# Clustered attention, dense layer and routed experts on one core: conversions respaced, preparation one step later, expert relu on one engine, two splits moved

## The chip, the cores and the metric

The program runs on one core of a Trainium2 chip. A core has five engines with a queue each that runs strictly in order: PE (TensorE, matrix products and transposes), DVE (VectorE), ACT (ScalarE), POOL (GpSimd) and SP (SyncE, which here only issues DMA transfers). Engines wait for one another through semaphores. The metric is the device time of one launch in microseconds (us), and lower is better.

## The reference

```python
def _attn_ref(q, k, v, centroids):          # q, k, v: 2 x 8 heads x 768 x 64; 16 centroids a head
    q_assign = np.argmax(np.einsum('bhsd,hcd->bhsc', q_n, c_n), axis=-1)   # and k_assign
    mask = q_assign[:, :, :, None] == k_assign[:, :, None, :]
    scores = np.where(mask, scale * np.matmul(q, k.transpose(0, 1, 3, 2)), -1000000000.0)
    attn = np.exp(scores - np.max(scores, axis=-1, keepdims=True))
    return np.matmul(attn / (np.sum(attn, axis=-1, keepdims=True) + 1e-09), v)
...
h = x @ w_in                                 # x: 1536 tokens x 512, w_in: 512 x 2048
x = np.maximum(0.01 * h, h) @ w_out          # w_out: 2048 x 512
...
# then 8 experts: each token with x @ w_skip > 0 goes to the expert with the largest logit
h = np.maximum(xc[mask] @ w1[e], 0.0)        # w1[e]: 512 x 1024
y[mask] = gate_w[mask, None] * (h @ w2[e])   # w2[e]: 1024 x 512
out[do_compute] = xc + y
```

`w_in` and `w_out` come as 64-bit floating-point numbers, and the kernel turns them into 32-bit ones itself.

## The kernel before

The kernel has three parts, and its order is written out by hand: the framework adds the semaphores but moves nothing, so the order of the code is the order on every engine.

**Attention.** Two heads form a pair, and there are 8 pairs with 12 steps each (96 steps, `s`; within a pair the step is `r`, within half a pair `rf`). One step computes the scores of 128 queries of one head (`st_scores`), takes their maximum on DVE, the exponential on ACT (`st_exp`), and, three steps later (`LAG`), transposes the result on PE (`st_transpose`, two PSUM buffers `tps`) and copies it out of PSUM on ACT (`st_evac`, tile `pt`). In every second step eight products with `v` follow (`st_av`). After each half of a pair `recip_rows` transposes the reciprocals of the row sums into one of the same two PSUM buffers (`rcps`), ACT copies them out, SP stores them, and `recip_load` on POOL's queue reads them back for `av_split`, which writes the attention output as a rounded part `xh` and a rest `xl`. While a pair is computed, the next ones are prepared: `raw_pe`/`raw_act` transpose q and k, `assign_*`, `argmax_*` and `mask_*` find the clusters. The tables `PREP`, `PREP0`, `PREP1` and `PREPS` give step and slot of each piece; `plan(d)` makes such a table, in which `d` is the step of the last argmax operation. The preparing products share one PSUM buffer.

**Conversion.** `w_in` and `w_out` come in 32 pieces. A piece is loaded (`load_piece`, tiles `stg`), and `convert_op` turns it with one operation on ACT (tile `cvu`) and four on DVE into 32-bit numbers. Twenty pieces are done during attention (`conv_step`), the last twelve in the first layer (`conv_next(n)`: convert, two pieces at a time, until `n` of the twelve are done).

**The first layer** goes over three blocks of 512 tokens (`NBLK`, `BT`) and in each over 16 slices of the hidden width (`NFC`); `i` counts all 48. Every operand is split into a rounded part and a rest, and three products stand for one. `m1_up(i)` makes 12 products into `ups`; `m1_act(i)` is the chain ACT `lk`, DVE `g`, ACT `gh`, DVE `gl`; `m1_down(i)` makes 12 products into `acc`. The weights of slice `i + 2` are split by `split_i(i + 2)` (ACT `whii`, then POOL `wloi`) and `split_o(i + 2)` (ACT `whio`, POOL `wloo`), which stand behind `m1_act(i)` in the code. The route of each block's tokens is computed beside it (`r_trans`, `r_part`, `r_logit`, `r_gen`).

**The experts.** The 36 weight pieces of 1 MB ("chunks") go through a ring of eight (`rawa` two, `rawb` six). An expert has four stages, two up (`up_half`) and two down (`down_half`); `split_stage(n)` splits the chunk of stage `n` into his two parts with two ACT copies and two subtractions (`split2`), writes them over the used `xh` and `xl`, and then asks for the next chunk (`refill`). Stage `n + 3` (`LEAD`) is split while PE computes stage `n`. After `up_half` the relu of half 0 is on ACT and that of half 1 on DVE; `h_trans` transposes it, ACT makes `hTh` and DVE `hTl`. `extras` and `tile_list` are some 60 small DVE operations between the first stages, which find the tokens that exceed one tile of 128.

## Time and profile before

| what | value |
|---|---|
| median of 3 runs | 690.68 us (690.42 to 690.96) |
| the profiled execution | 689.63 us, its span 687.9 us |
| PE / ACT / DVE / POOL busy, share of the span | 93% / 62% / 59% / 40% |
| attention / first layer / experts, by where their work stands in the trace | to 266 / 266 to 555 / 566 to 680 us |

The span reaches from the first to the last instruction of the profiled execution; the rest of its time, 1.73 us, lies outside. A busy PE is only an upper bound of its use, since the ends of its instructions are modelled; what counts is where it starts late and what released it.

### The profile page before, as it was taken

The numbers are of one execution on the slowest core, as the hardware profiler recorded it, in microseconds if no ns is written. First come the engines' busy times: TensorE is split into PE (matmuls) and PEld (weight loads), VectorE is DVE, ScalarE is ACT, GpSimd is POOL, SyncE is SP. The second block draws the span as 40 slices with busy tenths as digits, with TensorE's granted clock in tenths as the row PEclk, the third lists the DMA queues.
The fourth block names the chain that finished last, engine by engine and source line by source line (L and its number), as shares of the span: only waits on it lengthen the run. The fifth ranks groups of instructions, "written<-read, shape, count | busy, mean of one in ns | idle before, by whom it ended". The sixth has DMA issues, their size and how long they took to land. (4 is left out here: it accounts for less than half of the span.)

```text
span 687.9 us, 10140 instructions
## 1 busy us (share of the span) xinstructions
PE 636.7 (93%) x3587; PEld 491.8 (71%) x3587; DVE 407.4 (59%) x687; ACT 423.8 (62%) x824; POOL 278.2 (40%) x295
## 2 busy tenths in 40 slices
PE   5898999999999999499999999999999979989994
PEld 3676766666766666378888888788787868767873
DVE  5755858686776653767523213623226348999991
ACT  5887888897888885254445444445444436757870
POOL 4233636264553324363554444444444273002321
PEclk9999999999999999889999999999999999999997
DMA  8763764767656354221003000006303349989950
GB/s 196 184 189 95 196 163 140 187 172 193 167 153 171 111 183 144 104 111 61 1 3 122 1 1 0 1 0 245 122 3 122 123 163 362 339 280 333 357 192 25
DMA packets 62659, 98.31 MB, mean 143 GB/s; under 512 B 27593, under 2 KB 31659, under 8 KB 62224
## 3 DMA queue, kind: packets, MB, share of 16 engines
q1 hardware_dynamic: 59040, 88.13, 41.5%
q0 software_dynamic: 3568, 9.52, 4.2%
q8 instruction: 29, 0.48, 0.3%
q14 instruction: 22, 0.18, 0.1%
HBM read 72.47 MB, written 11.65 MB: 122 GB/s over the span
## 5 line engine op out<-in xcount | busy, mean ns | idle before, releaser
L369 DVE TENSOR_REDUCE st<-sps 128x1 f32<-128x768 f32 x96 | 91.5, 954 | 66.7 <-PE sps L366 66.3
L430 ACT ACTIVATE pt<-tps 128x384 f32<-128x384 f32 x192 | 84.8, 503 | 19.2 <-PE tps L423 18.6
L384 ACT ACTIVATE pr<-sps,st 128x768 f32<-128x768 f32 x96 | 87.7, 914 | 13.9 <-DVE st L369 13.4
L750 DVE TENSOR_TENSOR g<-ups,lk 128x512 f32<-128x512 f32 x48 | 33.1, 689 | 105.9 <-ACT lk L749 105.8
L634 POOL TENSOR_TENSOR wloi<-rawb,whii 128x512 fp32r<-128x512 f32 x36 | 46.7, 1298 | 115.4 <-ACT whii L632 115.4
L658 PE MATMUL ups<-xh,whii 128*128 128x512 f32 x192 | 76.0, 396 | 7.9 <-ACT whii L632 7.9
L423 PE MATMUL tps<-ident,pr 128*128 128x128 f32 x576 | 78.7, 273 | 0.5 <-ACT pt L430 0.5
L658 PE MATMUL ups<-xh,wloi 128*128 128x512 f32 x192 | 75.7, 394 | 1.4 <-POOL wloi L634 1.3
L658 PE MATMUL ups<-xl,whii 128*128 128x512 f32 x192 | 75.6, 394 | 0.0
L765 PE MATMUL acc<-whio,gh 128*128 128x512 f32 x184 | 73.4, 399 | 0.0
L765 PE MATMUL acc<-wloo,gh 128*128 128x512 f32 x184 | 71.8, 390 | 0.1
L423 PEld LDWEIGHTS tps<-ident,pr 128*128 128x128 f32 x576 | 68.4, 140 | 5.1 <-ACT pt L430 1.6
L438 PE MATMUL avps<-pt,vnat 128*64 128x384 f32 x384 | 71.9, 498 | 0.0
L765 PE MATMUL acc<-whio,gl 128*128 128x512 f32 x184 | 71.8, 390 | 0.0
L751 ACT ACTIVATE gh<-g 128x512 fp32r<-128x512 f32 x48 | 30.4, 632 | 51.9 <-DVE g L750 51.9
L749 ACT ACTIVATE lk<-ups 128x512 f32<-128x512 f32 x48 | 28.5, 593 | 50.9 <-PE ups L658 50.9
L752 DVE TENSOR_TENSOR gl<-g,gh 128x512 fp32r<-128x512 f32 x48 | 34.6, 721 | 33.5 <-ACT gh L751 33.5
L453 POOL TENSOR_TENSOR xr<-xr,rb 128x384 f32<-128x384 f32 x16 | 16.0, 1002 | 81.2 <-ACT xr L446 77.9
L658 PEld LDWEIGHTS ups<-xh,whii 128*128 128x128 f32 x192 | 36.6, 190 | 16.3 <-ACT whii L632 8.3
L644 POOL TENSOR_TENSOR wloo<-rawb,whio 128x512 fp32r<-128x512 f32 x36 | 47.0, 1304 | 0.8 <-ACT whio L643 0.8
L1171 POOL DMA_INDIRECT out_dram<-y,idx_s x8 | 13.6, 1695 | 76.8 <-DVE y L1169 36.0
L658 PEld LDWEIGHTS ups<-xh,wloi 128*128 128x128 f32 x192 | 36.6, 190 | 10.2 <-POOL wloi L634 2.6
(294 smaller groups left out, 1388.8 us busy)
## 6 DMA issues: line engine op xcount, KB each, us to landing
rawb<-in_moe_w_dram SPq DMA_DIRECT2D x26, 1024.0 KB, 6.9
stg<-in_moe_w_in_dram SPq DMA_DIRECT2D x16, 512.0 KB
stg<-in_moe_w_out_dram SPq DMA_DIRECT2D x16, 512.0 KB, 6.8
rawa<-in_moe_w_dram SPq DMA_DIRECT2D x8, 1024.0 KB
vnat<-in_v_dram SPq DMA_DIRECT2D x8, 384.0 KB, 3.7
rb<-recip_scratch POOLq DMA_DIRECT2D x32, 96.0 KB, 3.0
w_f_scratch<-cvt SPq DMA_DIRECT2D x12, 256.0 KB, 2.3
rawb<-w_f_scratch SPq DMA_DIRECT2D x3, 1024.0 KB
```

The source lines that it names most:

```text
L369: nc.vector.tensor_reduce(out=st[:, 0:1], in_=ps[:, :, 0:HS], axis=AX.XY, op=ALU.max, negate=True)
L384: nc.scalar.activation(out=pr, in_=ps[:, :, 0:HS], func=AF.Exp, bias=st[:, 0:1], accum_out=sm_t[g][:, 3 * h + j:3 * h + j + 1])
L423: nc.tensor.transpose(ps[:, t, :], pr[:, kh, t * P:(t + 1) * P], ident)
L430: nc.scalar.activation(out=pt[:, 3 * kh:3 * kh + 3, j, :], in_=t_t[s][kh], func=AF.Copy)
L438: nc.tensor.matmul(av_t[g][64 * h:64 * h + 64, :], lhsT=vnat[p][:, h, kt, :], rhs=pt_t[p, half, h][:, kt].rearrange("p j c -> p (j c)"), s ...
L634: eng.tensor_tensor(out=lo, in0=src, in1=_f(hi), op=ALU.subtract)
L644: nc.gpsimd.tensor_tensor(out=lo, in0=src, in1=_f(hi), op=ALU.subtract)
L658: nc.tensor.matmul(ps, lhsT=w[:, cc, :], rhs=x[:, cc, cs], start=(n == 0), stop=(n == 3 * KD - 1))
L750: nc.vector.tensor_tensor(out=g, in0=ps, in1=t, op=ALU.max)
L751: nc.scalar.activation(out=gh, in_=g, func=AF.Copy)
L752: nc.vector.tensor_tensor(out=gl, in0=g, in1=_f(gh), op=ALU.subtract)
L765: nc.tensor.matmul(ps, lhsT=a[:, ts_], rhs=w, start=(fc == 0 and n == 0), stop=(fc == NFC - 1 and n == 2))
```

## The change

1. `plan(0)` becomes `plan(1)` for the pairs 4 to 7, `plan(4)` becomes `plan(5)` for pair 2 and `plan(2)` becomes `plan(3)` for pair 3: transposes, assignment and argmax of the next pair stand one step later. `recip_rows` and the store of its row also stand one step later (`rf` 3 and 4 instead of 2 and 3).
2. `xh` and `xl` are laid out by block instead of by token. `av_split` makes two pieces of each half pair that crosses a block's edge (8 of 16 halves).
3. The twelve pieces left for the first layer are converted two each at `i` = 1, 3, 5, 7, 8, 9. Before it was four at `i` = 1 and two each at 3, 5, 7, 9.
4. Stages 0 and 1 of the experts are split at `i` = 37 and 40 of the first layer, with DVE's subtraction in place of POOL's, and their chunks' successors are loaded there by SP. Stage 2 takes the place of stage 0 behind the layer (POOL), stage 3 that of stage 2 (DVE). The chunks 12 and 13 are loaded ahead of 10 and 11.
5. Both halves of the experts' relu are on ACT.
6. The one-hot matrix of `tile_list` is made by 4 DVE operations over three tiles instead of 12 over one.

```diff
@@ -320,12 +320,12 @@
             (3, "d", exchange, 0), (5, "d", exchange, 1), (max(d + 2, 5), "d", mask_dma, None),
         ]
 
-    PREP = plan(0)
+    PREP = plan(1)
     PREP0 = [(3, "a0", assign_act, None), (3, "pb", argmax_pe, None), (4, "d", argmax_0, None), (4, "d", argmax_1, None),
              (5, "d", argmax_2, None), (6, "d", argmax_3, None)]
     PREP1 = [(1, "pb", assign_pe, None), (2, "a0", assign_act, None), (2, "pb", argmax_pe, None), (3, "pb", argmax_0, None), (4, "pb", argmax_1, None), (5, "d", argmax_2, None), (6, "pb", argmax_3, None), (7, "pb", mask_pe, None), (8, "d", mask_dve, None),
              (8, "d", mask_dma, None)]
-    PREPS = {0: PREP0, 1: PREP1, 2: plan(4), 3: plan(2)}
+    PREPS = {0: PREP0, 1: PREP1, 2: plan(5), 3: plan(3)}
 
     def prep(p, r, slot):
         if p >= NP:
@@ -341,8 +341,11 @@
 
     NP = B * NPAIR
 
-    xh = xpool.tile([P, KD, NTOK], F32R, name="xh")
-    xl = xpool.tile([P, KD, NTOK], F32R, name="xl")
+    NBLK = 3
+    BT = NTOK // NBLK
+    TPB = BT // P
+    xh = xpool.tile([P, NBLK, KD, BT], F32R, name="xh")
+    xl = xpool.tile([P, NBLK, KD, BT], F32R, name="xl")
 
     NSTEP = B * NPAIR * 12
     rcs = [att.tile([P, P], F32, name=f"rc{i}") for i in range(2)]
@@ -448,11 +451,18 @@
     def av_split(g):
         p, half = divmod(g, 2)
         b, cc = divmod(p, NPAIR)
-        cs = slice(b * S + half * HS, b * S + (half + 1) * HS)
         xr = xr_t.pop(g)
         nc.gpsimd.tensor_tensor(out=xr, in0=xr, in1=rrow_t.pop(g), op=ALU.mult)
-        nc.gpsimd.tensor_scalar(out=xh[:, cc, cs], in0=xr, scalar1=1.0, scalar2=1.0, op0=ALU.mult, op1=ALU.mult)
-        nc.gpsimd.tensor_tensor(out=xl[:, cc, cs], in0=xr, in1=_f(xh[:, cc, cs]), op=ALU.subtract)
+        n0 = b * S + half * HS
+        cuts = sorted({n0, n0 + HS} | {n for n in range(0, NTOK, BT) if n0 < n < n0 + HS})
+        parts = []
+        for a, z in zip(cuts, cuts[1:]):
+            blk = a // BT
+            cs = slice(a - blk * BT, z - blk * BT)
+            parts.append((xr[:, a - n0:z - n0], xh[:, blk, cc, cs], xl[:, blk, cc, cs]))
+        for src, hi, lo in parts:
+            nc.gpsimd.tensor_scalar(out=hi, in0=src, scalar1=1.0, scalar2=1.0, op0=ALU.mult, op1=ALU.mult)
+            nc.gpsimd.tensor_tensor(out=lo, in0=src, in1=_f(hi), op=ALU.subtract)
 
     def first_copy(i):
         nm = "qk"[i // 2]
@@ -617,9 +627,6 @@
                 if m + 2 < NPC:
                     load_piece(*divmod(m + 2, 4))
 
-    NBLK = 3
-    BT = NTOK // NBLK
-    TPB = BT // P
     NFC = DFF // P
     wq_i, wq_o = {}, {}
 
@@ -651,11 +658,10 @@
         whi, wlo = wq_i.pop(i)
         if ps is None:
             ps = bank("up", 2, "ups")
-        cs = slice(blk * BT, (blk + 1) * BT)
         n = 0
         for cc in range(KD):
             for w, x in ((whi, xh), (whi, xl), (wlo, xh)):
-                nc.tensor.matmul(ps, lhsT=w[:, cc, :], rhs=x[:, cc, cs], start=(n == 0), stop=(n == 3 * KD - 1))
+                nc.tensor.matmul(ps, lhsT=w[:, cc, :], rhs=x[:, blk, cc, :], start=(n == 0), stop=(n == 3 * KD - 1))
                 n += 1
         up_t[i] = ps
 
@@ -689,9 +695,9 @@
             st_evac(s - LAG)
         gf, rf = divmod(s, 6)
         if 0 < gf <= NSTEP // 6:
-            if rf == 2:
+            if rf == 3:
                 recip_rows(gf - 1)
-            elif rf == 3:
+            elif rf == 4:
                 nc.sync.dma_start(rscr[gf - 1], rrow_t.pop(gf - 1))
         g, kt = divmod(s - 6 - LAG, 6)
         if 0 <= g < NSTEP // 6 and kt % 2:
@@ -960,8 +966,8 @@
         V.tensor_scalar(out=g, in0=g, scalar1=1.0 / 1024.0, scalar2=None, op0=ALU.mult)
 
 
-    xhb = xh.rearrange("p c n -> p (c n)").rearrange("p (k a f) -> p k a f", a=2, f=512)
-    xlb = xl.rearrange("p c n -> p (c n)").rearrange("p (k a f) -> p k a f", a=2, f=512)
+    xhb = xh.rearrange("p b c n -> p (b c n)").rearrange("p (k a f) -> p k a f", a=2, f=512)
+    xlb = xl.rearrange("p b c n -> p (b c n)").rearrange("p (k a f) -> p k a f", a=2, f=512)
     NXB = KD * NTOK // 1024
     his, los = [xhb[:, k_] for k_ in range(NXB)], [xlb[:, k_] for k_ in range(NXB)]
     pc_t = {}
@@ -1035,19 +1041,21 @@
             m1_down(i - 2)
         m1_act(i)
         step_gen(i, 1)
+        if i in (2 * NFC + 5, 2 * NFC + 8):
+            split_stage((i - 2 * NFC) // 8)
         if i + 2 < NI:
             if i:
                 split_i(i + 2)
             split_o(i + 2)
             g_, j_ = divmod(i + 2 - 2 * NFC, 4)
             if g_ >= 0 and j_ == 3:
-                load_chunk(8 + 2 * g_)
-                load_chunk(9 + 2 * g_)
-        conv_next(i + 3 if i % 2 else 0)
+                for c in ((8, 9), (12, 13), (10, 11), (14, 15))[g_]:
+                    load_chunk(c)
+        conv_next({1: 2, 3: 4, 5: 6, 7: 8, 8: 10, 9: 12}.get(i, 0))
 
     lb = NBLK - 1
     LT = lb * TPB
-    split_stage(0, hold=True, pool_n=range(8))
+    split_stage(2, hold=True, pool_n=range(8))
     for t in range(TPB):
         ts_ = slice(t * P, (t + 1) * P)
         for i in (NI - 2, NI - 1):
@@ -1062,8 +1070,6 @@
             r_logit(LT + t - 3)
         if t >= 2:
             r_part(LT + t - 2)
-        if t == 0:
-            split_stage(1, hold=True, pool_n=range(8))
     r_trans(LT + TPB - 1, "up", 2)
     r_logit(LT + TPB - 3)
     r_part(LT + TPB - 2)
@@ -1101,9 +1107,7 @@
     for n, i in enumerate(order):
         gather(i, idx_g[:, pos_of[i]:pos_of[i] + 1])
         if n == 1:
-            refill(8, nc.gpsimd)
-            refill(9, nc.gpsimd)
-    split_stage(2, pool_n=())
+            refill(12, nc.gpsimd)
     m1.release()
     wip[0].release()
 
@@ -1112,6 +1116,8 @@
     for k_ in range(2):
         his.append(m2.tile([P, 2, 512], F32R, name=f"phi{k_}"))
         los.append(m2.tile([P, 2, 512], F32R, name=f"plo{k_}"))
+
+    split_stage(3)
 
     def x_prep(e):
         ps = bank("misc", 1, "xT", [P, KD, P])
@@ -1133,9 +1139,7 @@
             nc.tensor.matmul(ps, lhsT=x[:, c, :], rhs=w, start=(n == 0), stop=(n == 3 * KD - 1))
         if h == 0:
             h_t[e] = m2.tile([P, 2, 512], F32, tag="h", name="h", bufs=2)
-            nc.scalar.activation(out=h_t[e][:, 0, :], in_=ps, func=AF.Relu)
-        else:
-            nc.vector.tensor_scalar(out=h_t[e][:, 1, :], in0=ps, scalar1=0.0, scalar2=None, op0=ALU.max)
+        nc.scalar.activation(out=h_t[e][:, h, :], in_=ps, func=AF.Relu)
 
     def h_trans(e, h):
         ps = bank("up", 2, "hT", [P, 4, P])
@@ -1201,10 +1205,11 @@
         V.tensor_tensor(out=vx, in0=vv, in1=bc(sel.unsqueeze(2), [P, NTT, 5]), op=ALU.mult)
         yield
         ohx = m2.tile([P, NTT, P], F16, tag="ohx", name="ohx")
-        for t in range(NTT):
-            V.tensor_scalar(out=ohx[:, t], in0=iota, scalar1=jt[:, 1, t:t + 1], scalar2=None, op0=ALU.is_equal)
-            if t % 2:
-                yield
+        q = NTT // 4
+        for t in range(0, NTT, q):
+            V.tensor_tensor(out=ohx[:, t:t + q], in0=bc(iota.unsqueeze(1), [P, q, P]),
+                            in1=bc(jt[:, 1, t:t + q].unsqueeze(2), [P, q, P]), op=ALU.is_equal)
+            yield
         for _ in range(8):
             yield
         ps = bank("up", 2, "xps", [P, 5, 1])
@@ -1365,7 +1370,8 @@
             xx_gather()
         if n == 22:
             xx_prep()
-        split_stage(n + LEAD)
+        if n:
+            split_stage(n + LEAD)
         if (k_, i, h) == ("u", last, 1):
             pass
```

On ACT at the start of the first layer, the rows are the chain of slice 1 and what follows up to the weights of slice 4 (`cvu` is the first operation of a converted piece, `whii` the rounded weights). Before:

```order
L751 ACTIVATE gh<-g 128x512
L632 ACTIVATE whii<-rawa 128x512
L643 ACTIVATE whio<-rawa 128x512
L557 ACTIVATE cvu<-stg 128x512 x2
L557 ACTIVATE cvu<-stg_3385 128x512
L557 ACTIVATE cvu<-stg 128x512
L749 ACTIVATE lk<-ups 128x512
L751 ACTIVATE gh<-g 128x512
L632 ACTIVATE whii<-rawb 128x512
```

and with the change:

```order
L757 ACTIVATE gh<-g 128x512
L639 ACTIVATE whii<-rawa 128x512
L650 ACTIVATE whio<-rawa 128x512
L567 ACTIVATE cvu<-stg 128x512 x2
L755 ACTIVATE lk<-ups 128x512
L757 ACTIVATE gh<-g 128x512
L639 ACTIVATE whii<-rawb 128x512
```

The second pair of conversions, which stood ahead of slice 2's `lk`, is gone from here. It comes back at `i` = 8 and 9, where the change has three groups of conversions in successive slices:

```order
L567 ACTIVATE cvu<-stg_3579 128x512
L567 ACTIVATE cvu<-stg 128x512
L755 ACTIVATE lk<-ups 128x512
L757 ACTIVATE gh<-g 128x512
L639 ACTIVATE whii<-rawb 128x512
L650 ACTIVATE whio<-rawb 128x512
L567 ACTIVATE cvu<-stg_3680 128x512
L567 ACTIVATE cvu<-stg 128x512
L755 ACTIVATE lk<-ups 128x512
```

In these rows two successive slices both carry a group; before, one slice without a group always lay between two with one.

On PE in the second half of pair 3, the rows are steps 8 and 9 (`sps` scores, `tps` transposes of the exponentials, `rcps` the reciprocals, `avps` products with v, `asps` the assignment). Before:

```order
L423 MATMUL tps<-ident,pr 128x128 x6
L401 MATMUL rcps<-ident,rc_114 128x128
L438 MATMUL avps<-pt_1712,vnat 64x384
L438 MATMUL avps<-pt_1739,vnat 64x384
L438 MATMUL avps<-pt_1712,vnat 64x384
L438 MATMUL avps<-pt_1739,vnat 64x384
L231 MATMUL asps<-raw,cblk 32x384 x4
L366 MATMUL sps<-UB 128x384 x2
```

and with the change:

```order
L441 MATMUL avps<-pt_1740,vnat 64x384
L179 MATMUL rawps<-ident,natk 128x128 x3
L369 MATMUL sps<-UB 128x384 x2
L369 MATMUL sps<-VB 128x384 x2
L426 MATMUL tps<-ident,pr 128x128 x6
L404 MATMUL rcps<-ident,rc_114 128x128
L231 MATMUL asps<-raw,cblk 32x384 x4
L369 MATMUL sps<-UA 128x384 x2
```

`rcps` and the assignment moved from step 8, which has products with v, to step 9, which has none; the last `rawps` moved from step 7 into step 8.

## Rows read from the trace of the kernel before

**Rows 1.** The page: the span.

```profile
span 687.9 us, 10140 instructions
```

**Rows 2.** Five stretches: length, busy time and instructions of each engine, granted clock, DMA share.

```profile
40.00:255.00 215.00, 202.75 (x1337) 145.10 (x1336) 148.96 (x222) 179.81 (x411) 96.45 (x124) 1.00 0.59 160
...
290.00:296.00 6.00, 2.79 (x6) 1.78 (x7) 3.78 (x7) 3.36 (x7) 2.52 (x2) 0.50 0.50 175
...
340.00:540.00 200.00, 199.55 (x967) 162.41 (x966) 66.96 (x134) 88.24 (x160) 91.48 (x88) 1.00 0.15 54
590.00:626.00 36.00, 32.65 (x161) 24.91 (x160) 35.66 (x74) 24.92 (x31) 3.02 (x3) 1.00 0.90 304
629.00:663.00 34.00, 34.00 (x189) 27.20 (x188) 32.66 (x36) 25.70 (x33) 11.15 (x4) 1.00 0.95 336
```

**Rows 3.** Waits of the whole span: us in total, times, longest.

```profile
PE rcps L401 <- ACT pt L430: 11.0, 16, 1.1
```

**Rows 4.** Timeline of PE, 280 to 310 us: start, length, idle time before it.

```profile
293.08 0.79 PE L658 MATMUL ups<-xh,whii 128*128 128x512 f32 x1 [7.90 <-ACT whii L632]
...
298.59 0.39 PE L765 MATMUL acc<-whio,gh 128*128 128x512 f32 x1
...
301.31 0.39 PE L658 MATMUL ups<-xh,whii 128*128 128x512 f32 x1
```

**Rows 5.** Timeline of ACT, 254 to 300 us.

```profile
287.05 0.66 ACT L557 ACTIVATE cvu<-stg 128x512 f32<-128x512 f32 x1 [6.22 <-DMA stg<-in_moe_w_out_dram]
287.61 0.59 ACT L749 ACTIVATE lk<-ups 128x512 f32<-128x512 f32 x1
291.88 0.63 ACT L751 ACTIVATE gh<-g 128x512 fp32r<-128x512 f32 x1 [3.68 <-DVE g L750]
292.42 0.61 ACT L632 ACTIVATE whii<-rawb 128x512 fp32r<-128x512 f32 x1
```

**Rows 6.** Timeline of DVE, 254 to 305 us.

```profile
276.00 2.72 DVE L559 TENSOR_SCALAR cvu<-cvu 128x512 f32<-128x512 f32 x2
...
282.69 1.28 DVE L570 SCALAR_TENSOR_TENSOR rawb<-stg,cvt 128x512 uint32<-128x512 uint32 x2
...
291.16 0.68 DVE L750 TENSOR_TENSOR g<-ups,lk 128x512 f32<-128x512 f32 x1
```

**Rows 7.** Timeline of POOL, 254 to 305 us.

```profile
293.10 1.27 POOL L634 TENSOR_TENSOR wloi<-rawb,whii 128x512 fp32r<-128x512 f32 x1 [11.83 <-ACT whii L632]
```

**Rows 8.** Timeline of ACT, 296 to 342 us: one cycle of conversions.

```profile
307.49 1.20 ACT L557 ACTIVATE cvu<-stg 128x512 f32<-128x512 f32 x2
...
313.80 0.63 ACT L751 ACTIVATE gh<-g 128x512 fp32r<-128x512 f32 x1 [3.47 <-DVE g L750]
...
317.83 0.63 ACT L643 ACTIVATE whio<-rawb 128x512 fp32r<-128x512 f32 x1
318.37 1.22 ACT L557 ACTIVATE cvu<-stg 128x512 f32<-128x512 f32 x2
```

**Rows 9.** Timeline of DVE, 296 to 342 us.

```profile
308.17 1.91 DVE L559 TENSOR_SCALAR cvu<-cvu 128x512 f32<-128x512 f32 x2 [1.11 <-ACT cvu L557]
...
313.08 0.68 DVE L750 TENSOR_TENSOR g<-ups,lk 128x512 f32<-128x512 f32 x1
```

**Rows 10.** Waits between 590 and 626 us.

```profile
PE yps L1162 <- DVE hTl L1147: 1.6, 2, 1.2
...
PE yps L1162 <- DVE xl L978: 0.8, 1, 0.8
```

**Rows 11.** Groups by line of the whole span: busy us, mean ns, idle before.

```profile
L978 DVE TENSOR_TENSOR xl<-rawb,xh 128x1024 fp32r<-128x1024 f32 x36 | 42.3, 1215 | 0.3 <-ACT xh L976 0.3
...
L1138 DVE TENSOR_SCALAR h<-hps 128x512 f32<-128x512 f32 x8 | 5.4, 680 | 0.0
...
L1205 DVE TENSOR_SCALAR ohx<-iotax,jt 128x128 f16<-128x128 f32 x12 | 2.5, 293 | 0.0
```

**Rows 12.** Timeline of PE, step 8 of pair 3.

```profile
128.41 0.33 PE L401 MATMUL rcps<-ident,rc 128*128 128x128 f32 x1 [1.13 <-ACT pt L430]
```

**Rows 13.** Timeline of ACT, step 8 of pair 3: the work ahead of that product.

```profile
126.94 0.66 ACT L557 ACTIVATE cvu<-stg 128x512 f32<-128x512 f32 x1
```

**Rows 14.** Timeline of DVE, pair 1.

```profile
54.32 0.55 DVE L263 TENSOR_REDUCE mx<-eq 128x24 f32<-128x384 f32 x1 [2.41 <-POOL eq L258]
```

## The prediction

> **What bounds the kernel now.** I read the page, then the stretches, the waits, and last the timelines around the places where PE starts late.
>
> The span is 687.9 us [rows 1]. The stretches [rows 2] show that almost all of it is PE: 202.75 of 215 us in attention, 199.55 of 200 us in the body of the first layer. There the other engines have time to spare, and moving their work does nothing by itself. PE loses time in three places, and these are what the change can reach.
>
> First, at the start of the first layer. PE waits 7.90 us for the rounded weights `whii` of slice 4, and then works slowly: its twelve products take from 293.08 to 298.59 us, 5.5 us, while the next twelve take 2.7 us, to 301.31 [rows 4]. The granted clock is 0.50 between 290 and 296 us [rows 2], the lower of the two levels (1.2 GHz), after an engine that had stood still. The chain behind the wait is read backwards: `whii` is queued on ACT behind `gh`, `gh` waits for DVE's `g`, and `g` stands on DVE behind eight conversion operations for the third and fourth piece; ACT itself could not begin the fourth, because its load had not landed until 287.05 (6.22 us of idleness) [rows 5, 6].
>
> Second, in the experts. Between 590 and 626 us DVE is busy for 35.66 of 36 us, PE for 32.65, so 3.35 us of PE are lost [rows 2]. PE waits for DVE's `hTl` and for the rests of the weights [rows 10]. Later, from 629 to 663 us, PE is full again.
>
> Third, in attention: PE's 16 `rcps` transposes wait 11.0 us in all for ACT to empty a `tps` buffer [rows 3].
>
> **The change part by part.**
>
> *Conversions.* With only two pieces at `i` = 1, DVE is done with them at 282.69 + 1.28 = 283.97 us [rows 6] and can do slice 2's `g` then instead of at 291.16, 7.2 us earlier. `gh` and `whii` follow by the same 7.2 us, and PE starts slice 4 at 293.08 - 7.2 = 285.9 us. PE is then idle for under 1.5 us at a time, a gap after which this trace shows no fall of the clock (it fell only behind the 7.90 us), so I count the twelve products at 2.7 us. POOL's `wloi` takes 1.27 us behind `whii` [rows 7], and the third product needs it; two products of about 0.23 us go ahead of it, so some 0.9 us is waited there. Slice 4 ends at 285.9 + 2.7 + 0.9 = 289.5 instead of 298.6 us: 9.1 us gained.
>
> Part of it is given back. One cycle of conversions, from a `cvu` to the next one two slices later, takes 318.37 - 307.49 = 10.88 us on ACT and DVE [rows 8]; PE's two slices take four times 2.72 us [rows 4], 10.88 too. So a conversion in every second slice just keeps pace. In a slice with a conversion the chain is: `cvu` to DVE's first operation 0.68 (307.49 to 308.17), DVE's eight operations 4.91 (to 313.08), `g` to `gh` 0.72 (to 313.80) [rows 8, 9], and `gh`, `whii`, `whio` at 0.54 us each to the next `cvu` [rows 5, 8], together 7.9 us. PE's slice takes 5.4 us. The change has groups at `i` = 7, 8 and 9, each queued behind the one before: ACT's `cvu` stands ahead of the next slice's `lk`, DVE's operations ahead of the next `g`, and PE waits for the `whii` behind them. Twice 7.9 - 5.4 makes 5.0 us of new waiting near `i` = 10 and 11. How much of it a lead covers is open, between nothing given back and all 5.0; I take all, because PE, restarted early, runs right behind `whii`, while in the trace of before the slow clock had let the chain get ahead. The early finish of all conversions is worth nothing in itself, as the last pieces are converted at `i` = 9 either way.
>
> *Smaller pieces of `xh`.* Eight halves cost POOL two more operations each. POOL is busy for 96.45 of 215 us in attention [rows 2], which hides them, except for the last such half: POOL's queue leads from there into the weights of slice 3, for which PE waits anyway. I add 0.5 us by estimate, under half of one operation of 1.27 us. The product's operand is 512 columns in both layouts, so PE's cost is unchanged.
>
> *Stages 0 and 1 in the last block.* Four copies on ACT and four subtractions of 1.2 us [rows 11] on DVE go into a stretch where DVE is busy for 66.96 and ACT for 88.24 of 200 us and the DMA share is 0.15 [rows 2]. Queued behind them are the weights of slices 39 and 42 and the next `g`; two copies of about a microsecond are less than the PE work of one slice, 5.4 us, that lies ahead. I cost them at nothing; without that cover they would cost some 2 us each time. The chunks loaded there are 2 MB less for the experts, whose DMA share is 0.90 to 0.95. But no engine is shown waiting for a chunk, so this too is nothing. Loading 12 and 13 first only follows the order of use.
>
> *Relu.* DVE loses eight operations of 0.68 us [rows 11], ACT gains as many; ACT has 11 of 36 us free, and at this place it already waits for PE. DVE gets ahead by 0.6 us with each expert. The waits of the first one or two experts and the last go away; the longest, 1.2 and 0.8 us [rows 10], fall at about 608 to 610 us, where PE, no longer held up before, comes earlier by about as much as DVE does, so they mostly stay. I take 1.5 us, between 0 and the 3.35 us that PE loses there. Splitting stage 3 ahead of the first expert takes one chunk off DVE's queue later, but ACT's relu of half 1 then stands ahead of the next copy and takes most of that back.
>
> *One-hot matrix.* Twelve operations take 2.5 us [rows 11]. Four of 384 elements are shorter each than the 0.68 us of 512 elements, so at most 2.7 us: nothing either way.
>
> *Preparation and `rcps`, a step later.* In step 8 ACT does a conversion's `cvu` and a `raw` copy [rows 13] ahead of the `tps` copy, and PE waits 1.13 us [rows 12]. In step 9 a `raw` copy and the copy of the attention output take that place. I take 0.3 us off for each of five pairs, 1.5 us in all; but in pairs 1 and 2 the mask's product and its reading on DVE now meet the next pair's first transposes, which need the same PSUM buffer, in a step without products with v, where PE is early. I set that at the same 1.3 us and keep 0.2 us of gain. The bounds are wide: all 11.0 us of [rows 3], or a loss (below).
>
> **The sum**: -9.1 + 5.0 + 0.5 - 1.5 - 0.2 = -5.3 us. The profiled execution took 689.63 us, so 684.3; the median of the runs is 1.05 us above it, which makes **685.4 us**.
>
> **The rivals.**
>
> *Nothing is given back.* If the chain has a lead of 5 us at `i` = 8, the 9.1 stays, and if DVE's relief removes all 3.35 us and half a microsecond per pair goes in attention, 4 us: -9.1 + 0.5 - 3.35 - 4 = -16, 674.7 us. For it speaks that 0.68 us less of DVE in each expert lowers a queue that is 99% full. Against it speaks the equal period of 10.88 us: there is no spare rate from which a lead could come.
>
> *The conversions in successive slices slow down beside POOL.* The eight operations took 7.97 us at `i` = 1, 276.00 to 283.97 us [rows 6], with POOL subtracting all the while, and 4.91 us later. If the groups at `i` = 8 and 9 cost 8.0 us as well, PE waits 2 x 3.1 = 6.2 us more: +0.9 us, 691.6 us, no change that can be told. Against it: POOL has only 2.6 us of work in a slice. The Trainium skill, "GPSIMD Engine Reference", section 8, says that POOL shares its SBUF interfaces with VectorE and contends with instructions in a two-port mode or with two SBUF inputs. By this rule, the two-input subtractions moved to DVE at `i` = 37 and 40 would stretch as well; the trace agrees for the first conversion operation, whose two take 2.72 us beside POOL and 1.91 us with less of it.
>
> *Slower: the argmax chain holds up DVE.* In pair 1 DVE stood for 2.41 us before the second reduction of the argmax, waiting for POOL's product [rows 14], with the scores' maxima queued behind it. That order arises when the first reduction comes late. The change puts it into step 11, a short one. If DVE stands as long in each of pairs 2 to 6, and PE with it, that is 5 x 2.41 = 12 us, and -5.3 + 12 = +6.7, 697.4 us. It decides from about 1.1 us of PE for each pair. Against it: POOL stood idle there in the later pairs, and a maximum is needed only three steps later.
>
> **How the numbers follow.** The forecast has a chance of 0.60, with its own range 681 to 689 us; nothing given back 0.18, the slowed conversions 0.14, the argmax chain 0.08. A difference of 0.2%, 1.4 us, is about what a measurement of this kernel can tell from no change. Faster gets nearly all of the first, the second and a fifth of the third, 0.80; the same 0.10; slower 0.10. The range of eight in ten is 676 to 692 us: it leaves out the far end of the first rival and the last one.
>
> **What the profile after would show.** The wait before slice 4 under 1.5 us, and no fall of the clock there; new waits of PE for `whii` of about 1.6 us each at two slices some 40 to 50 us after the layer's start; PE's loss in the experts down to about 2 us; 16 waits for `rcps` of about 10 us. The prediction is wrong if the waits at `i` = 10 and 11 are missing, or if a pair in attention takes a microsecond more or less than before.

## The result, and the profile after

The changed kernel takes 684.41 us (median of 3 runs, 683.33 to 684.60) against 690.68 us, a ratio of 0.9905 (95% interval 0.9882 to 0.9927): faster by about 0.9%. The prediction was 685.4 us, in a range of 676 to 692. The profiled execution's span went from 687.9 us [rows 1] to 682.3 us.

The total was nearly right, but not all of its terms were. The table splits a span at the same events in each kernel. Each number is the difference of two starts in the timeline of PE: the first scores (`sps`), the first product of the first layer (`ups`), the first product of slices 10 and 13, the first transpose for the experts (`xT`), and the first product of the second half of the first and of the start of the sixth expert (`hps`).

| stretch, us | before | after | difference |
|---|---|---|---|
| start to first scores | 18.23 | 17.91 | -0.32 |
| attention: first scores to first `ups` | 248.27 | 244.52 | -3.75 |
| first layer: to slice 10 | 62.01 | 53.12 | -8.89 |
| slice 10 to slice 13 | 16.32 | 22.97 | +6.65 |
| slice 13 to first `xT` | 221.92 | 221.95 | +0.03 |
| first `xT` to the first expert's second half | 4.74 | 6.40 | +1.66 |
| from there to the sixth expert | 58.39 | 57.64 | -0.75 |
| from there to the end | 58.06 | 57.75 | -0.31 |

The sum of the last column is -5.68 us, the difference of the two spans but for rounding.

Waits of PE over the whole span after the change (us in total, times, longest):

```profile
PE rcps L404 <- ACT pt L433: 6.9, 15, 1.0
...
PE ups L664 <- ACT whii L639: 3.2, 3, 1.3
PE ups L664 <- POOL wloi L641: 3.1, 4, 1.3
...
PE yps L1166 <- DVE hTl L1151: 1.2, 1, 1.2
...
PE yps L1166 <- DVE xl L984: 1.1, 1, 1.1
```

The 7.90 us of [rows 4] are gone. What is left of them, and what came in their place, is in the timeline of PE from 275 to 339 us:

```profile
275.91 0.50 PE L664 MATMUL ups<-xh,wloi 128*128 128x512 f32 x1 [1.28 <-POOL wloi L641]
281.82 0.50 PE L664 MATMUL ups<-xh,whii 128*128 128x512 f32 x1 [0.63 <-ACT whii L639]
283.17 0.50 PE L664 MATMUL ups<-xh,wloi 128*128 128x512 f32 x1 [0.62 <-POOL wloi L641]
...
322.50 0.50 PE L664 MATMUL ups<-xh,whii 128*128 128x512 f32 x1 [1.26 <-ACT whii L639]
323.86 0.50 PE L664 MATMUL ups<-xh,wloi 128*128 128x512 f32 x1 [0.63 <-POOL wloi L641]
...
330.43 0.50 PE L664 MATMUL ups<-xh,whii 128*128 128x512 f32 x1 [1.29 <-ACT whii L639]
331.78 0.50 PE L664 MATMUL ups<-xh,wloi 128*128 128x512 f32 x1 [0.62 <-POOL wloi L641]
```

Slice 4 starts at 281.82 us after a wait of 0.63 us. At slices 11 and 12 PE waits anew, first for `whii` and then for `wloi`. Stretches of the changed kernel (length, busy time and instructions of PE, PE's weight loads, DVE, ACT and POOL, then the granted clock, the DMA share and GB/s):

```profile
40.00:255.00 215.00, 205.72 (x1357) 145.69 (x1356) 146.06 (x225) 179.84 (x418) 105.53 (x138) 1.00 0.61 162
280.00:286.00 6.00, 4.75 (x20) 3.31 (x19) 2.90 (x5) 4.63 (x9) 3.76 (x3) 1.00 0.69 262
319.00:333.00 14.00, 10.20 (x41) 7.12 (x40) 10.14 (x17) 6.29 (x12) 5.23 (x4) 0.99 0.01 1
333.00:340.00 7.00, 7.00 (x26) 5.63 (x25) 1.90 (x3) 3.20 (x6) 4.10 (x4) 0.78 0.00 0
...
557.00:564.00 7.00, 5.58 (x24) 5.03 (x24) 2.72 (x8) 0.66 (x2) 5.73 (x6) 0.50 0.77 256
585.00:621.00 36.00, 33.67 (x164) 26.77 (x163) 35.30 (x66) 26.37 (x34) 3.88 (x3) 0.95 0.90 305
```

The clock no longer falls at slice 4: it is 1.00 between 280 and 286 us, where it was 0.50 in the same place before [rows 2]. But it falls where it had not: to 0.78 on average behind the new waits (333 to 340 us), to 0.50 around the experts' start, and within 585 to 621 us. In the 36 us of the experts PE is idle for 36 - 33.67 = 2.33 us, 3.35 us before; that isn't all gain, since its products were slower for a part of them (the clock is 0.95 there, 1.00 before [rows 2]).

### The profile page after: what moved, and what is told of

The parts are those of the page before. It is cut to its first block, busy times and chain, and to the rows that moved or that the text cites. A ratio compares the mean times of both kernels' runs of the same rounds, so it can differ in the third digit from the quotient of the medians.

```text
span 682.3 us, 10130 instructions
## 1 busy us (share of the span) xinstructions
PE 639.5 (94%) x3587; PEld 492.8 (72%) x3587; DVE 403.5 (59%) x673; ACT 423.8 (62%) x832; POOL 279.6 (41%) x308
## 5 line engine op out<-in xcount | busy, mean ns | idle before, releaser
L641 POOL TENSOR_TENSOR wloi<-rawb,whii 128x512 fp32r<-128x512 f32 x36 | 48.1, 1336 | 111.4 <-ACT whii L639 111.4
L1175 POOL DMA_INDIRECT out_dram<-y,idx_s x8 | 11.0, 1375 | 81.4 <-DVE y L1173 50.1
L984 DVE TENSOR_TENSOR xl<-rawb,xh 128x1024 fp32r<-128x1024 f32 x34 | 40.0, 1219 | 4.3 <-ACT xh L982 4.0
```

The source lines that it names most:

```text
L641: eng.tensor_tensor(out=lo, in0=src, in1=_f(hi), op=ALU.subtract)
L984: eng.tensor_tensor(out=lo, in0=src, in1=_f(hi), op=ALU.subtract)
```

## The experiments

Ratios are to the kernel before on the same chip, with 95% intervals. Each kernel's own stretches follow in one table at the end of this section.

### Conversions in every second slice

```
-        conv_next({1: 2, 3: 4, 5: 6, 7: 8, 8: 10, 9: 12}.get(i, 0))
+        conv_next({1: 2, 3: 4, 5: 6, 7: 8, 9: 10, 11: 12}.get(i, 0))
```

> The changed kernel with the conversions in every second slice (i = 1, 3, 5, 7, 9, 11, two pieces each) instead of at 1, 3, 5, 7, 8, 9. Theory: the 6.7 us that the changed kernel gives back between the twelve products of slices 10 and 13 come from groups in successive slices, whose chain (7.9 us) is longer than PE's slice (5.4 us). In every second slice chain and PE have the same period of 10.9 us, so the waits of PE for whii at slices 11 and 12 and the fall of the clock at 332 us go away: some 6.7 us less than the changed kernel, 677 to 678 us. Rival one: PE without any lead waits at every second slice instead, since the periods are only equal; about half is given back all the same, near 681 us. Rival two: what is given back has another cause (POOL's rests wloi), and the time stays at 684 us. Rival three: the last two pieces, converted at i = 11 now, are late for slice 14, a new wait of one chain, about 8 us with a fall of the clock: no gain on the changed kernel.

Measured: 678.04 us, ratio 0.9819 (0.9804 to 0.9835). Slices 10 to 13 take 16.36 us instead of 22.97. These are the waits of PE on the weights between 260 and 340 us, in all:

```profile
PE ups L664 <- POOL wloi L641: 1.9, 2, 1.3
PE ups L664 <- ACT whii L639: 0.6, 1, 0.6
```

They are those of slices 3 and 4; there is none at slices 11 and 12. So what was given back came from groups in successive slices and from nothing else. The first rival is out too: with equal periods PE, restarted early, runs on without waiting.

### The conversions alone

The kernel before, with the changed kernel's `conv_next({1: 2, 3: 4, 5: 6, 7: 8, 8: 10, 9: 12}.get(i, 0))` as its one edit.

> The kernel before with the new places of the conversions alone (i = 1, 3, 5, 7, 8, 9). Theory: the first layer is shorter by what the changed kernel shows there, 9.0 us gained at slice 4 less 6.7 us given back at slices 11 to 13, so 2.2 us less than before, 688.5 us (687.5 to 689). By the prediction's own terms (-9.1 + 5.0) it would be 686.6 us. Rival: the smaller pieces of xh or the shifted preparation in attention have a part in what is gained at slice 4 or given back; then this kernel differs from the 2.2 us by more than 1.5 us, either way.

Measured: 688.70 us, ratio 0.9973 (0.9962 to 0.9984). Up to slice 10 it is 9.03 us faster than before (62.01 to 52.98), and from there to slice 13 it loses 5.03 us (16.32 to 21.35). The waits at 322 to 340 us are the same as in the changed kernel, with a granted clock of 1.00:

```profile
322.00:340.00 18.00, 14.15 (x59) 10.46 (x58) 12.47 (x20) 7.80 (x15) 7.79 (x6) 1.00 0.00 1
```

The same waits cost 5.03 us here and 6.65 us in the changed kernel. The rest, 1.62 us, is the clock: it stayed up here and fell there. The gain of the median, 690.35 to 688.70, is 1.7 us, within the theory's range. The profiled execution, in which the clock stayed up there, is the second fastest of the eleven and 3.5 us below the profiled one of before; whether the clock fell at slices 11 and 12 in the others isn't shown.

### The preparation alone, the `rcps` transposes alone

First kernel: `PREP = plan(1)` and `2: plan(5), 3: plan(3)` put into the kernel before, and nothing else. Second kernel: the kernel before with

```
-            if rf == 2:
+            if rf == 3:
                 recip_rows(gf - 1)
-            elif rf == 3:
+            elif rf == 4:
                 nc.sync.dma_start(rscr[gf - 1], rrow_t.pop(gf - 1))
```

> The kernel before with the preparation of pairs 2 to 7 moved a step later and nothing else. The changed kernel's attention is 4.06 us shorter (from the start to the first products with the experts' first layer). Theory: most of this comes from the rcps transposes and not from here; the preparation alone gives -1.3 us in pair 1 and +1.3 us in pair 2, and within 1 us of nothing in all: 689.7 to 691.7 us. Rival: the preparation gives most of the 4 us: 686.7 to 687.7 us.

Measured: 691.09 us, ratio 1.0009 (1.0000 to 1.0018), no gain. Pair 0 is 0.97 us shorter, pair 1 is 0.81 us shorter (33.79 to 32.98) and pair 2 is 1.58 us longer (31.34 to 32.92); attention as a whole is 0.28 us longer.

> The kernel before with the rcps transposes and the store of their row a step later and nothing else. Theory: steps 8 and 9 of a pair together took 6.94 us before and 6.25 us in the changed kernel, and it is the rcps transpose, no longer behind a conversion's copy and a raw copy on ACT, that gives this: 0.4 to 0.5 us in each of eight pairs, 3 to 4 us in all, 686.7 to 687.7 us. Rival one: the prediction's figure, 0.3 us for five pairs, 1.5 us: 689.2 us. Rival two: the preparation gives the 4 us, this one nothing: 690.7 us.

Measured: 683.72 us, ratio 0.9909 (0.9894 to 0.9924). This one edit gains as much as the whole change, and nearly twice what the theory said: attention goes from 248.27 to 241.76 us. PE's waits for `rcps` in attention:

```profile
PE rcps L401 <- ACT pt L430: 5.1, 15, 0.6
```

11.0 us before [rows 3], 5.1 us now: 5.9 of the 6.5 us. The same product in pair 3, now in step 9, waits 0.25 us where it waited 1.13 us [rows 12]:

```profile
129.61 0.33 PE L401 MATMUL rcps<-ident,rc 128*128 128x128 f32 x1 [0.25 <-ACT pt L430]
```

And ACT in that step, for comparison with [rows 13]:

```profile
127.78 0.57 ACT L446 ACTIVATE xr<-avps 128x384 f32<-128x384 f32 x1
128.15 0.59 ACT L237 ACTIVATE sc<-asps 128x384 f32<-128x384 f32 x1
129.06 0.87 ACT L430 ACTIVATE pt<-tps 128x384 f32<-128x384 f32 x2 [0.33 <-PE tps L423]
```

Here ACT stands idle for 0.33 us until PE has written `tps`: it is ahead of PE, and `rcps` waits only for the copies themselves.

### `rcps` two steps later

The kernel with the spread conversions and the old preparation (next but one), with `rf == 4` and `rf == 5`.

> The kernel with the conversions in every second slice and the old steps of the preparation (674.2 us), with the rcps transposes and the store two steps later than before instead of one. Theory: PE's wait at rcps is set by what ACT has queued ahead of the tps copies in that step. In steps 4 and 10 of a pair ACT has a conversion's copy (step 4) or nothing but the scores (step 10) ahead, so one half gets better and one worse, and attention stays within 1 us of 241.6 us (from the first scores to the first product of the layer): 674.2 us within 1 us. Rival: any later step is better, since rcps is then surely behind nothing, another 3 us or more: 671 us. The other way: in even steps, which have the products with v, PE is queued fuller and the waits of before (1.1 us each) come back: 680 us.

Measured: 682.63 us, ratio 0.9893 (0.9876 to 0.9910), by the time the third of the three answers, though not for its reason. Attention is 249.70 us, 8.1 us longer than with the product one step earlier, and PE waits more for `rcps` than ever:

```profile
PE rcps L404 <- ACT pt L433: 12.0, 15, 1.8
```

Pair 3 shows where. In step 4 the product waits 1.09 us, in step 10 only 0.25:

```profile
118.60 0.33 PE L404 MATMUL rcps<-ident,rc 128*128 128x128 f32 x1 [1.09 <-ACT pt L433]
...
134.62 0.33 PE L404 MATMUL rcps<-ident,rc 128*128 128x128 f32 x1 [0.25 <-ACT pt L433]
```

ACT ahead of the `tps` copies of step 4:

```profile
117.49 0.67 ACT L567 ACTIVATE cvu<-stg 128x512 f32<-128x512 f32 x1
118.05 0.88 ACT L433 ACTIVATE pt<-tps 128x384 f32<-128x384 f32 x2
118.97 0.27 ACT L406 ACTIVATE rrow<-rcps 6x128 f32<-6x128 f32 x1
```

A conversion's `cvu` stands there, as in step 8 before; in step 10 there is none. The lengths of the steps agree. In pair 3 steps 9 and 10 take 5.28 us together with `rcps` in the one or in the other (2.30 + 2.98, 1.72 + 3.56), while steps 3 and 4 go from 5.24 to 6.08 us. It is the same in the other pairs: the seven waits in step 4 are 1.08 to 1.78 us long, those in step 10 0.25 to 0.68; and in the kernel before the waits in step 8 of pairs 1 to 6 are 1.09 to 1.13 us, those in step 2 0.25 to 0.54. So it is the `cvu` ahead of the `tps` copies that makes the wait long, and the odd steps are good because they have none. The theory had this cause, but it took step 10 to gain what step 4 loses, and the wait in step 9 was short already.

### The preparation taken back

The kernel with the spread conversions, with `PREP = plan(0)`, `plan(4)` and `plan(2)` again.

> The kernel with the conversions in every second slice (678.0 us), with the preparation of pairs 2 to 7 back in the steps of before and the rcps transposes left a step later. Alone on the kernel before, the rcps transposes took 6.4 us from attention and the moved preparation added 1.2 us. Theory: the preparation's shift is a loss in the changed kernel too, 4.06 us gained there against 6.41 us without it, so 2.3 us less: 675.7 us. Rival: of this 2.3 us, 1.2 us are the preparation and the rest is the eight halves of xh in two pieces; then 676.8 us. The other way: the two shifts belong together, and the preparation in its old steps now meets the rcps row on ACT: 678 us or more.

Measured: 674.24 us, ratio 0.9779 (0.9757 to 0.9801). Attention is 241.64 us against 244.53: the moved preparation costs 2.9 us where `rcps` is moved as well, ten times what it costs alone. Pair 2 is 2.25 us shorter without it (32.60 to 30.35), pairs 3 to 5 0.6 us each and pair 6 0.2 us; pair 0 is 1.33 us longer. In the changed kernel pair 2 has a wait that this kernel doesn't have:

```profile
89.03 0.52 PE L179 MATMUL rawps<-ident,natq 128*128 128x128 f32 x3 [1.36 <-issue]
```

These are the next pair's first transposes, which use the PSUM buffer of the mask's product (`ohps`). The row names no releaser, but DVE reads that product just before, to 88.93 us:

```profile
88.26 0.67 DVE L296 TENSOR_SCALAR mk<-ohps,msc 128x384 fp32r<-128x384 bf16 x1
```

In pairs 3 to 5 the wait for `rcps` in step 3 is 0.72 us in the changed kernel and 0.25 with the old preparation. ACT's exponential ahead of it waits longer for DVE's maximum `st`. In pair 3 of the changed kernel:

```profile
110.66 0.51 DVE L268 TENSOR_TENSOR oh<-eq,mx 128x384 bf16<-128x384 f32 x1
...
113.21 0.90 ACT L387 ACTIVATE pr<-sps,st 128x768 f32<-128x768 f32 x1 [1.19 <-DVE st L372]
```

and with the old preparation:

```profile
111.52 0.90 ACT L387 ACTIVATE pr<-sps,st 128x768 f32<-128x768 f32 x1 [0.32 <-DVE st L372]
```

On DVE the argmax's last operation (`oh`) now stands directly ahead of that maximum but for one operation of a conversion, and there is no pause between them; with the old preparation it stood one maximum earlier, and DVE had a pause of 0.83 us behind it. That this is what delays the maximum is read from these rows and was not tried.

Since 241.64 us is also what `rcps` alone gives (241.76), with `xh` in one piece, the smaller pieces of `xh` cost nothing.

### Stages 0 and 1 put back; the two edits alone

The changed kernel without the two `split_stage` calls at `i` = 37 and 40, with the load order, the split of stages 0 to 2 behind the last block and the refills of before.

> The changed kernel with the experts' first stages split where they were before (after the last block, the first copies held, the chunks loaded in the order 8 to 15) and nothing else. Prediction: this part costs and brings nothing, 684.4 us within 0.5 us. Rival one: the 1.7 us that the changed kernel loses between the gathers and the second half of the first expert, where the granted clock stays at 0.5 for 10.2 us instead of 3.4 us, comes with this part, and without it the kernel takes 682.7 us. Rival two: the early split gives DVE a lead in the experts, and without it PE waits 1 us more: 685.4 us.

Measured: 683.13 us, ratio 0.9896 (0.9874 to 0.9919). No stretch of it differs from the changed kernel's by more than 0.3 us. The part costs and brings nothing.

Then the kernel before with only `rf` 3 and 4 and the spread conversions:

> The kernel before with two edits alone: the rcps transposes and the store of their row a step later, and the conversions in every second slice (i = 1, 3, 5, 7, 9, 11). The pieces of xh, the split stages, the relu, the one-hot matrix and the preparation are those of before. Theory: these two edits are nearly all that can be gained: 6.4 us in attention and 9.0 us in the first layer, 15.4 us less than before, 674.9 us by the median of before shown first (a ratio of 0.978). Rival: the experts' edits bring their predicted 1.5 us, and this kernel is that much slower than the one that has them too (674.2 us, a ratio of 0.9779), at a ratio of 0.980.

Measured: 676.46 us, ratio 0.9799 (0.9783 to 0.9816). Two edits give two per cent, twice what the whole change gives. Theory and rival lie 0.2% apart, and the intervals of this kernel and of the one that has the experts' edits too (0.9757 to 0.9801) overlap: the times don't tell the two answers apart. The profiled executions have the same span, 672.2 us each, since the kernel with the edits lost more to the low clock at the first expert. Whether the experts' edits bring something is left to the next kernels, which look at the relu by itself.

### The relu, and the clock around the experts

Half 1's relu back on DVE, in the changed kernel:

```
+            nc.scalar.activation(out=h_t[e][:, 0, :], in_=ps, func=AF.Relu)
+        else:
+            nc.vector.tensor_scalar(out=h_t[e][:, 1, :], in0=ps, scalar1=0.0, scalar2=None, op0=ALU.max)
-        nc.scalar.activation(out=h_t[e][:, h, :], in_=ps, func=AF.Relu)
```

> The changed kernel with the relu of the experts' second half back on DVE and nothing else. Theory: from 590 to 626 us DVE is the full engine again, PE waits for hTl and the rests of the weights at each expert, and 0.7 to 1.5 us come back: 685.1 to 685.9 us. Rival: ACT's relu of the second half costs as much as DVE's did, since the next copies of the weights stand behind it, and the time is 684.4 us within 0.4 us. That the kernel gets faster (683.5 us or less) would say that the relu on ACT is a loss.

Measured: 683.53 us, ratio 0.9913 (0.9897 to 0.9929): not to be told from the changed kernel by the time. Its trace is no better a judge as it stands, since the clock fell at other places in it: not behind slices 11 and 12, but longer in the experts.

So the clock was tried next: more products of the identity (`keep_busy`) in PE's pauses ahead of the experts.

```
-    for _ in range(5):
-        next(gl_)
+    next(gl_)
+    keep_busy(6)
+    next(gl_)
+    keep_busy(4)
+    for _ in range(3):
+        next(gl_)
     keep_busy(8)
```

> The changed kernel with ten more products of the identity by itself on PE, six before the pos products and four before the sidx products, in the two pauses of 1.38 and 0.83 us that lie right before the granted clock falls at 554.5 us; they write a buffer that nobody reads. Theory: PE stands still for under 0.6 us there, the clock doesn't fall, and the 1.66 us that are lost until the second half of the first expert come back: 682.7 us. Rival: the clock falls all the same behind the later pause of 1.42 us before the first xT (560.5 us), the first expert's products are slow instead, and the time stays at 684.4 us or goes up by the extra products, up to 685.4 us.

Measured: 683.32 us, ratio 0.9905 (0.9885 to 0.9926), the rival. The stretches of this kernel, where the pauses of 1.38 and 0.83 us are filled:

```profile
553.00:557.00 4.00, 3.96 (x36) 3.39 (x35) 3.59 (x15) 1.59 (x2) 1.36 (x1) 1.00 0.00 0
557.00:560.00 3.00, 0.03 (x1) 0.00 (x0) 0.85 (x1) 0.00 (x0) 2.52 (x3) 1.00 0.46 126
560.00:564.00 4.00, 3.85 (x16) 3.57 (x16) 1.83 (x8) 0.66 (x2) 2.95 (x4) 0.57 1.05 385
```

At full speed PE is done sooner and then stands for 3 us until the first gather lands; the clock is up until 560 us and down, 0.57, from there. The slow clock had hidden how long that pause is. So in the next kernel (on the one with spread conversions and old preparation) all pauses are filled: as above with `keep_busy(22)` for the last, and, in the third expert's `down_half`,

```
                 for n, (x, w) in enumerate(((hi, whi), (hi, wlo), (lo, whi))):
+                    if (e, h, f) == (order[2], 0, 0) and n:
+                        keep_busy(5)
                     nc.tensor.matmul(ps[:, cs], lhsT=x[:, f, :], rhs=w[:, cs], start=(h == 0 and f == 0 and n == 0),
```

> The kernel with the conversions in every second slice and the old steps of the preparation (674.2 us), with products of the identity by itself in all pauses of PE around the experts' start: six before pos, four before sidx, fourteen more while the first gather is awaited (3.1 us at the full clock), and five each before the two products of the third expert that wait for xl and hTl. Theory: with no pause of PE left over 0.6 us the clock falls neither at 544 nor at 595 us; the first expert takes 4.7 us from its first transposes to the second half instead of 6.0 us, and 1.2 us come back behind the third expert: 671.7 us. Rival one: the falls come all the same and the time stays at 674.2 us. Rival two: the added products end behind the values that they wait with and delay the true ones, 1 to 2 us more: 675 to 676 us.

Measured: 672.47 us, ratio 0.9744 (0.9729 to 0.9759), the best of all kernels here. The clock is 1.00 in these stretches:

```profile
546.00:551.00 5.00, 4.95 (x47) 4.66 (x47) 4.25 (x14) 1.36 (x2) 2.30 (x2) 1.00 0.01 3
551.00:558.00 7.00, 6.98 (x51) 6.04 (x50) 3.35 (x17) 1.56 (x4) 5.47 (x7) 1.00 0.97 338
575.00:611.00 36.00, 35.87 (x193) 29.29 (x192) 35.62 (x66) 26.77 (x35) 3.88 (x3) 1.00 0.89 311
```

The two stretches at the experts take 4.47 and 56.05 us, where they took 6.02 and 57.62: the 1.6 us of each are what the low clock cost there. At the third expert the two kernels keep step up to the products that ran at the low clock (595.5 to 598.5 us without the filling), and 1.5 of the 1.57 us arise in these. By the times alone the gain is small, since the two intervals touch.

With the clock up, the relu can be seen by itself: the same kernel with half 1's relu on DVE.

> The kernel with products in the pauses, as above, and the relu of the experts' second half back on DVE. It is to show the relu's share by itself, with as little of the clock in it as can be. Theory: PE waits again by 0.5 to 0.9 us for hTl at two of the first experts and by 0.5 us at the argument of the last, 1.0 to 1.5 us more than with the relu on ACT: 672.7 to 673.2 us. Rival: DVE isn't what PE waits for in most of them, and the difference is under 0.4 us. As the changed kernel with its relu on DVE took no longer by the median, the relu on ACT could also be a loss: then this kernel is the faster one of the two.

Measured: 674.47 us, ratio 0.9767 (0.9753 to 0.9781), 2.0 us more than with the relu on ACT, and more than the theory's 1.0 to 1.5. The stretch from the first expert's second half to the sixth expert takes 57.97 instead of 56.05 us. PE waits for DVE again, at three places where the other kernel has no wait:

```profile
PE yps L1174 <- DVE nxi L1270: 0.5, 1, 0.5
...
PE yps L1174 <- DVE hTl L1157: 0.2, 1, 0.2
PE yps L1174 <- DVE exi L1203: 0.2, 1, 0.2
```

That is 0.9 of the 1.9 us. The timeline of PE has all of it: at four places, three of them these waits, a product with `hTl` starts 0.32, 0.67, 0.33 and 0.16 us later behind the one ahead of it than in the other kernel, and the one behind it takes another 0.11 us each time, 1.92 us in all.

### All kernels by stretch

Differences of starts in PE's timeline, us, as in the first table. "1 to 6" is from the first expert's second half to the sixth expert. In brackets: how long the granted clock was at 0.5 in that stretch, or just ahead of it.

| kernel | attention | to slice 10 | 10 to 13 | first `xT` to second half | 1 to 6 |
|---|---|---|---|---|---|
| before | 248.27 | 62.01 (10.2) | 16.32 | 4.74 (3.4) | 58.39 |
| changed | 244.52 | 53.12 | 22.97 (3.4) | 6.40 (10.2) | 57.64 (3.4) |
| conversions alone | 248.07 | 52.98 | 21.35 | 4.55 (6.8) | 59.17 (3.4) |
| preparation alone | 248.55 | 61.73 (10.2) | 16.32 | 4.53 (3.4) | 59.13 |
| `rcps` alone | 241.76 | 61.87 (10.2) | 16.32 | 4.55 (3.4) | 59.01 |
| spread conversions | 244.53 | 52.90 | 16.36 | 6.31 (10.2) | 57.63 (3.4) |
| and old preparation | 241.64 | 52.86 | 16.40 | 6.02 (10.2) | 57.62 (3.4) |
| and `rcps` two later | 249.70 | 53.73 | 16.37 | 4.48 (6.8) | 57.67 (3.4) |
| stages put back | 244.28 | 53.30 | 22.93 (3.4) | 6.31 (10.2) | 57.68 (3.4) |
| relu on DVE | 244.57 | 52.89 | 21.35 | 5.93 (10.2) | 59.97 (6.8) |
| two pauses filled | 244.62 | 52.91 | 21.39 | 5.99 (3.4) | 57.63 (3.4) |
| two edits alone | 241.91 | 53.04 | 16.39 | 4.54 (6.8) | 58.62 (3.4) |
| all pauses filled | 243.56 (3.4) | 53.13 | 16.39 | 4.47 | 56.05 |
| that, relu on DVE | 243.55 (3.4) | 52.92 | 16.45 | 4.47 | 57.97 |

Attention is 1.9 us longer in the last two kernels than in the one that they start from: 0.6 us of it in pair 0, where the clock was down for 3.4 us at 20 us, the rest in pairs 2 (0.5 us) and 5 (0.85 us). In step 3 of both the wait for `rcps` is longer by half a microsecond (1.25 against 0.72 us, 0.81 against 0.25), and ACT's exponential ahead of it waits longer for DVE's maximum; why DVE is late there isn't shown.

With the experts' code of before, which has the relu on DVE, the fall of 3.4 us at the third expert cost next to nothing: the stretch "1 to 6" takes 59.17 us with it (conversions alone) and 59.13 without (preparation alone). The products at the low clock lose 1.4 us there too, but 1.3 us come back behind them at three products with `hTl`, where PE then waits less. The fall of 6.8 us in the changed kernel with the relu on DVE does show (59.97 us, against 57.97 with all pauses filled).

## Why the prediction was right, and where it wasn't

The mechanism at slice 4 and its price were right, and so was what is given back as long as the clock stays up. That the total came out within 1 us is luck, since terms that were wrong nearly cancelled. Against the predicted -5.3 us stand -5.7 us: attention 3.6 us better (the start's 0.3 not counted), the first layer 1.4 us worse in slices 10 to 13 and at slice 4 together with the pieces of `xh`, and the experts 2.1 us worse.

**Conversions, -9.1 us.** Shown: -8.89 us here, -9.03 us with the conversions alone. The wait is 0.63 us and the clock stays at 1.00 there, as the profile was to show.

**Given back, +5.0 us.** The step was right: two cycles of 7.9 us against slices of 5.4 us. DVE's first conversion operations in the changed kernel start 7.99 and 7.96 us apart:

```profile
307.61 2.01 DVE L569 TENSOR_SCALAR cvu<-cvu 128x512 f32<-128x512 f32 x2 [0.85 <-ACT cvu L567]
...
315.60 1.99 DVE L569 TENSOR_SCALAR cvu<-cvu 128x512 f32<-128x512 f32 x2 [0.91 <-ACT cvu L567]
...
323.56 1.96 DVE L569 TENSOR_SCALAR cvu<-cvu 128x512 f32<-128x512 f32 x2 [0.91 <-ACT cvu L567]
```

Where the clock stayed up the loss was 5.03 us (conversions alone, relu on DVE: 21.35 against 16.32). Where it fell, 6.65 us. The waits came at slices 11 and 12, 60 and 68 us after the layer's start, not at 10 and 11 and 40 to 50 us after it: a group of conversions delays the weights three slices on. What failed is the sentence that PE idle for under 1.5 us shows no fall of the clock. It was false of the trace of before already: there the clock was 0.5 for 3.4 us from 561.09 us on, behind pauses of 1.38 and 0.83 us, which the prediction had not looked at. PE of the kernel before, and the stretch behind it with its clock of 0.57:

```profile
559.83 0.19 PE L898 MATMUL pos<-oh,ltri 128*128 128x32 f16 x1 [1.38 <-DVE oh L895]
...
560.94 0.78 PE L920 MATMUL sidx<-rv,ohs 128*128 128x8 f16 x4 [0.83 <-DVE ohs L916]
```

```profile
561.00:565.00 4.00, 3.97 (x20) 3.52 (x20) 3.08 (x7) 0.16 (x1) 2.48 (x2) 0.57 0.05 6
```

The rival that nothing is given back is refuted by these rows, and that the cycle slows down beside POOL by the 7.96 us. Its basis was also read too widely: in the kernel before POOL subtracts only up to 281.27 us, and of the eight operations from 276.00 to 283.97 us only the first four are longer than in the later cycle (2.72 and 2.92 us for two each, later 1.91 and 0.75); the last four take 1.28 us for two in both.

**Pieces of `xh`, +0.5 us.** Nothing: attention is the same with and without them, and slice 3's wait for `wloi` is 1.28 us in the changed kernel, 1.29 before. The term had no wait as its basis.

**Attention, -0.2 us.** The largest error, -3.75 us measured. Of its two halves the gain was set too low: 0.3 us for each of five pairs, because in step 9 other copies would take the place of the `cvu`. Alone it is 6.5 us over eight pairs. The bound that was named, the 11.0 us of [rows 3], was the better guide: a good half of it went away, since ACT in the odd steps has no `cvu` and is ahead of PE. The loss was set at 1.3 us for pairs 1 and 2; the new wait came in pair 2 alone, at 1.36 us, at the place foreseen, while pair 1 had one of 0.90 us before, which grew to 1.12. But the moved preparation costs 2.9 us in all on top of `rcps`: 2.25 us in pair 2, 0.6 in each of pairs 3 to 5, which the prediction had as nothing, and 0.2 in pair 6, less the 1.3 us that it gains in pair 0. Of the two signs that the prediction named for its being wrong, the one in attention came: pair 1 takes 1.31 us less than before and pair 2 1.26 us more. PE waits 15 times for `rcps`, 6.9 us in all, not 16 times and about 10.

**Experts, -1.5 us.** The relu by itself is worth 1.9 to 2.0 us with the clock up, somewhat more than was said. In the changed kernel this was not to be seen: from the first `xT` to the end it takes 121.79 us against 121.19, because 1.6 us were lost to a longer stretch of the low clock at the first expert and about as much in the third. The stages and the one-hot matrix at nothing: shown for the stages; the one-hot matrix was not tried alone, but its four operations take 2.0 us where the twelve took 2.5 [rows 11].

**DVE held up by the argmax.** Not at the size that was feared: no pair from 3 on is longer than before, and pair 2's 1.26 us come with the new wait of 1.36 us above. In small it may have come: in pairs 3 to 5, where the argmax's last operation stands ahead of DVE's maximum, the moved preparation costs 0.6 us each.

What stays open is why the low clock lasted 10.2 us at the experts' start in some kernels and 3.4 or 6.8 us in others. It isn't the experts' code: the kernel with `rcps` two steps later has the same as the one with spread conversions and old preparation, 6.8 us against 10.2, and its products of the first expert ran at full speed.

## What to carry to other kernels

When work is moved into a stretch, write down the period of its chain and the period of the engine that waits for it, and lay it out at that period: six groups of conversions at the distance at which both take 10.9 us cost nothing, and the same six with three in a row gave back 5 of 9 us. Test two shifts of one schedule singly as well as together: the one edit of a step (`rcps`) was worth 6.5 us and the other, which cost 0.3 us alone, took nearly half of it away. Count every pause of the main engine, short ones too, and what the clock did behind it, before a wait is priced by its length alone; and ask whether a later wait gives the loss back.
